# Two tokens a partition and a quartered array for the first sequence, the whole array for the others, in a fused attention and MLP kernel

## The chip, the cores and the metric

The kernel runs on one core of a Trainium2 chip. The metric is the device time of one execution in microseconds (us); lower is better. Matmul operands are bf16, sums are f32.

## The reference, cut to what matters

The inputs are q, k and v of four sequences, eight heads, 768 tokens and 64 elements a head, a decay `lam` for each head, and two weight matrices. The first stage is linear attention with decay, in blocks of tokens; the second is an MLP over the 3072 tokens with a piecewise quadratic gate.

```python
# q, k, v: (4, 8, 768, 64); w_in: (512, 2048); w_out: (2048, 512)
for b in range(nb):                         # blocks of a sequence
    intra = einsum('bhic,bhjc->bhij', qb, kb) * Dmask          # lam ** (i - j), causal
    intra = einsum('bhij,bhjd->bhid', intra, vb)
    inter = einsum('bhid,bhde->bhie', qb * lam_pow, kv_state)
    out[:, :, sl] = intra + inter
    kv_state = lam_block * kv_state + einsum('bhsd,bhse->bhde', kb * rev_pow, vb)
x = out.transpose(0, 2, 1, 3).reshape(3072, 512)
h = x @ w_in
g = where(h >= 1, h, where(h <= -1, 0, (h + 1) ** 2 / 4))
return g @ w_out
```

The kernel works with blocks of 128 tokens in place of 64, which computes the same.

## The kernel before

**Tiles.** The 3072 tokens are cut into eight stripes (`STRIPES`, line 28): stripe 0 is the first 512 tokens of sequence 0 (four blocks, C = 4), stripe 1 its last 256 (C = 2), stripes 2 to 7 are the halves of the other sequences (C = 3, 384 tokens). A unit is a stripe s and a head pair hp (two heads of 64 elements fill 128 partitions); there are four units a stripe.

**Forms.** `FORMS = "pfffwwww"` (line 27) gives each stripe its way of doing attention. In all of them decayed copies of k and q are made in bf16, k and q are transposed so that heads lie on partitions, scores are k times q for each block, they are masked, the inner products multiply them with v, a state a block is built from k and v, and the carried part multiplies q with the state before it.

- p (stripe 0): transposes by TensorE (line 344), copied out of PSUM by ScalarE (lines 352, 354); scores on half the array's rows (line 372); inner products on half its columns (line 519), carried parts on quarters of it (line 538); states by one scan on VectorE (line 468).
- f (stripes 1 to 3): transposes by TensorE too; a copy of k and v with a zero middle (`kz`, `vc`), so that inner products use the whole array and come out transposed (lines 506, 527).
- w (stripes 4 to 7): k is laid into zero-padded tiles of 128 columns a head; one DMA transposes nine tiles (`kqT<-kq`); scores, inner products and carried parts use the whole array (lines 368, 513, 532); the result has tokens on partitions (`xn`) and is turned by a second DMA (`xT<-xn`).

**The MLP.** For a stripe of T tokens, `mlp_in` (line 595) makes one of 16 column blocks of h by four matmuls of T columns; for the first three blocks of stripe 0, `mlp_in_ko` (line 609) takes one head pair at a time, so that it can begin when the first unit is done. ScalarE adds 1 and clips below at 0 (line 618), VectorE makes the gate of four blocks by three instructions (lines 575 to 577), `mlp_out` (line 627) makes 128 tokens of the output by 16 matmuls of 512 columns in four parts, ScalarE copies them out (line 635) and SP stores them. The last 128 tokens are done in two column parts (line 647).

**Loads.** q, k and v come as f32 through SP's queue, in an order of its own, one block at a time (lines 160 to 166): for k and v a partition holds one token of a block, so that each row moved is 64 f32 (256 B); for q in forms p and f a partition holds C tokens of a head side by side. Raw tiles have two buffers each for q, k and v. Weights are loaded by GpSimd's queue with a cast to bf16, w_in in four column parts (W0 to W3, line 235) and w_out in four row parts (W4 to W7, line 239).

**The order.** The program is written out by hand in `ORDER` (lines 32 to 75), a list of words; each word issues instructions to its engines, and each engine runs its own in the order of the list. So a word whose operand is late holds all that stands behind it on its engine. The words that matter here, with s the stripe and p the head pair or part:

- L load, W weight load; `@` makes a load wait for another one's landing
- k, q, v: casts with decay; the last letter is the engine (a ScalarE, d VectorE, g GpSimd)
- T, Q: transposes of k and q (in form w, T is the DMA of both); t, u: their copies out of PSUM
- S scores, s mask, R state products, r state update, O inner products and carried parts, o copy out, X the DMA that turns `xn`
- K, P: first projection (P0a is stripe 0, block 10); h its ScalarE pass; A the gate of four blocks
- Y (stripe, 128 tokens, part): second projection, y copy out, U store, Z the last one
- D: warming matmuls without use; B masks; G, J zeros; E, b, z: copies that forms p and f need

## Time and profile before

| | us |
|---|---|
| runs of the kernel: lowest, median, highest | 220.54, 220.56, 220.89 |
| span of the profiled execution | 219.9 |
| TensorE busy | 209.4 |
| VectorE busy | 148.9 |
| ScalarE busy | 125.4 |
| GpSimd busy | 60.9 |

The profile is of one execution; times in it count from the start of its span. PE is TensorE, DVE VectorE, ACT ScalarE, POOL GpSimd, and SPq the queue from which SP issues DMAs. A line of a group names line, engine, operation, output and inputs, shape and count, then busy time and mean duration in ns, then the idle time of the engine ahead of it with what ended it. A line of the time line gives start, duration and the instructions merged. A line of a window gives its bounds, its length, each engine's busy time and count, the granted clock of TensorE (1.00 is full), the mean share of 16 DMA engines (over 1 when packets overlap) and GB/s.

### The profile page before, as it was taken

The numbers are of one execution on the slowest core, as the hardware profiler recorded it, in microseconds if no ns is written. First come the engines' busy times: TensorE is split into PE (matmuls) and PEld (weight loads), VectorE is DVE, ScalarE is ACT, GpSimd is POOL, SyncE is SP. The second block draws the span as 40 slices with busy tenths as digits, with TensorE's granted clock in tenths as the row PEclk, the third lists the DMA queues.
The fourth block names the chain that finished last, engine by engine and source line by source line (L and its number), as shares of the span: only waits on it lengthen the run. The fifth ranks groups of instructions, "written<-read, shape, count | busy, mean of one in ns | idle before, by whom it ended". The sixth has DMA issues, their size and how long they took to land.

```text
span 219.9 us, 4417 instructions
## 1 busy us (share of the span) xinstructions
PE 209.4 (95%) x1667; PEld 121.0 (55%) x1667; DVE 148.9 (68%) x239; ACT 125.4 (57%) x268; POOL 60.9 (28%) x122
## 2 busy tenths in 40 slices
PE   7488999999998999999999999999999999999994
PEld 2246445446765566555655666456655565555443
DVE  1387177971998789998499489936898649346700
ACT  3675689327983576874832686326655383256320
POOL 4376036007499810430311045003600000000000
PEclk9999999999999999999999999999999999999999
DMA  4999999999999993849999999899944222310103
GB/s 123 238 233 203 206 215 191 176 221 219 232 276 231 214 192 74 206 84 255 165 202 163 167 256 151 164 243 224 210 96 97 54 66 57 145 74 23 50 22 121
DMA packets 100629, 35.95 MB, mean 163 GB/s; under 512 B 89216, under 2 KB 97664, under 8 KB 100608
## 3 DMA queue, kind: packets, MB, share of 16 engines
q1 hardware_dynamic: 96384, 31.47, 69.0%
q0 software_dynamic: 4224, 4.19, 12.2%
q8 instruction: 13, 0.21, 0.4%
q14 instruction: 8, 0.07, 0.1%
HBM read 27.27 MB, written 6.29 MB: 153 GB/s over the span
## 4 chain that ended last, share of the span: by engine, by line
PE 85%; SPq 5%; DMA 5%; ACT 2%; issue 1%; POOL 1%; DVE 0%; DVEq 0%; ACTq 0%
PE ph L595 36%; PE py L627 34%; SPq L164 3%; DMA v_nat<-in_v_dram 3%; PE ps L368 2%; DMA xT<-xn 2%; PE pk L449 2%; PE py L647 2%; PE po L506 2%; PE pt L344 1%; PE ps L372 1%; PE ph L609 1%; PE po L513 1%; PE po L532 1%; SPq L166 1%; SPq L160 1%
## 5 line engine op out<-in xcount | busy, mean ns | idle before, releaser
L618 ACT ACTIVATE tt<-ph,one 128x384 bf16<-128x384 f32 (+2 forms) x128 | 70.5, 584 | 41.1 <-PE ph L595 29.5
L595 PE MATMUL ph<-xT,w_in_sb 128*128 128x384 bf16 (+2 forms) x500 | 93.1, 325 | 0.5 <-DMA xT<-xn 0.5
L627 PE MATMUL py<-w_out_sb,gT 128*128 128x512 bf16 x368 | 87.7, 379 | 0.0
L595 PEld LDWEIGHTS <-w_in_sb 128*128 128x128 bf16 x500 | 46.5, 98 | 30.5 <-issue 0.2
L627 PEld LDWEIGHTS <-gT 128*128 128x128 bf16 x368 | 34.5, 98 | 35.0 <-DVE sz L477 0.8
L389 DVE TENSOR_TENSOR sc<-ps,mask 128x768 bf16<-128x768 f32 (+1 forms) x28 | 25.6, 914 | 11.9 <-PE ps L368 11.6
L576 DVE TENSOR_TENSOR tt<-tt,mm 128x1536 bf16<-128x1536 bf16 (+2 forms) x32 | 32.6, 1019 | 1.1
L577 DVE TENSOR_TENSOR gT<-tt,mm 128x1536 bf16<-128x1536 bf16 (+2 forms) x32 | 32.0, 998 | 1.2
L575 DVE TENSOR_SCALAR mm<-tt 128x1536 bf16<-128x1536 bf16 (+2 forms) x32 | 19.7, 616 | 18.5 <-ACT tt L618 17.7
L315 POOL TENSOR_SCALAR kq<-k_nat,dec 128x192 bf16<-128x192 f32 (+2 forms) x36 | 19.6, 556 | 24.9 <-DMA k_nat<-in_k_dram 24.8
L635 ACT COPY osb<-py 128x512 f32<-128x512 f32 x23 | 13.5, 585 | 20.4 <-PE py L627 16.0
L320 POOL TENSOR_TENSOR kq<-q_nat,dec 128x384 bf16<-128x384 f32 (+1 forms) x15 | 13.2, 891 | 28.5 <-DMA q_nat<-in_q_dram 15.2
L477 DVE SCALAR_TENSOR_TENSOR sz<-sz,lam_blk,pk 128x128 bf16<-128x128 bf16 x48 | 16.4, 347 | 3.5 <-PE pk L449 2.2
L297 POOL CAST vc<-v_nat 128x384 bf16<-128x384 f32 (+1 forms) x15 | 9.3, 629 | 31.6 <-DMA v_nat<-in_v_dram 15.6
L344 PE MATMUL pt<-ident,kq 128*128 128x128 bf16 x96 | 9.4, 220 | 3.2 <-ACT kq L311 2.4
L548 ACT CAST xn<-po 128x384 bf16<-128x384 f32 x16 | 7.7, 478 | 5.3 <-PE po L532 5.2
L550 ACT CAST xT<-po 128x384 bf16<-128x384 f32 (+2 forms) x16 | 7.5, 483 | 5.5 <-PE po L527 3.6
L475 DVE CAST sz<-pk 128x128 bf16<-128x128 f32 x12 | 3.4, 285 | 10.0 <-PE pk L449 10.0
L344 PEld LDWEIGHTS <-kq 128*128 128x128 bf16 x96 | 6.5, 98 | 6.6 <-ACT kq L311 2.9
L295 ACT CAST vc<-v_nat 128x512 bf16<-128x512 f32 (+2 forms) x9 | 4.9, 549 | 8.9 <-DMA v_nat<-in_v_dram 8.9
L352 ACT COPY kqT<-pt 128x384 bf16<-128x384 bf16 (+2 forms) x16 | 7.7, 482 | 2.6 <-PE pt L344 2.6
L583 PE MATMUL pw<-ident 128*128 128x512 bf16 x23 | 7.5, 450 | 1.4 <-POOL ident masks.py:199 1.4
(79 smaller groups left out, 163.0 us busy)
## 6 DMA issues: line engine op xcount, KB each, us to landing
out_dram<-osb SPq DMA_DIRECT2D x23, 256.0 KB, 3.0
q_nat<-in_q_dram SPq DMA_DIRECT2D x18, 256.0 KB, 4.5
k_nat<-in_k_dram SPq DMA_DIRECT2D x24, 128.0 KB, 4.7
v_nat<-in_v_dram SPq DMA_DIRECT2D x24, 128.0 KB, 4.4
k_nat<-in_k_dram SPq DMA_DIRECT2D x12, 256.0 KB, 4.9
v_nat<-in_v_dram SPq DMA_DIRECT2D x12, 256.0 KB, 5.1
w_in_sb<-in_moe_w_in_dram POOLq DMA_DIRECT2D x4, 512.0 KB, 9.3
w_out_sb<-in_moe_w_out_dram POOLq DMA_DIRECT2D x4, 512.0 KB, 9.1
```

The costliest lines, as they stand in the source:

```text
L315: nc.gpsimd.tensor_scalar(dst[:, hi, :, :], src[:, hi, :, :], dec[:, row, 2 * hp + hi:2 * hp + hi + 1], 0.0, AX.mult, AX.add)
L320: (nc.gpsimd if eng == "g" else nc.vector).tensor_tensor(dst, src, decay(row, 2 * hp, C, inner), op=AX.mult)
L344: nc.tensor.transpose(out=d["pt"][:, i, c, :], in_=d["kq"][:, i * C + c, :], identity=ident)
L389: nc.vector.tensor_tensor(out=d["sc"][:, :, 0:C, :], in0=d["ps"][:, :, 0:T].rearrange("p h (c i) -> p h c i", c=C), in1=_ins(mask[:, 2 * h ...
L477: nc.vector.scalar_tensor_tensor(out=d["ss"][:, c, :], in0=prev, scalar=lam_blk[:, hp:hp + 1], in1=kv, op0=AX.mult, op1=AX.add)
L575: nc.vector.tensor_scalar(mm, tt, 0.5, 1.0, AX.mult, AX.min)
L576: nc.vector.tensor_tensor(tt, tt, mm, op=AX.subtract)
L577: nc.vector.tensor_tensor(g[:, 4 * a:4 * a + 4, 0:T], tt, mm, op=AX.mult)
L595: nc.tensor.matmul(ph[:, 0:T], lhsT=w_in_sb[:, ko, ni * 128:(ni + 1) * 128], rhs=x_tiles[s][:, ko, 0:T], start=(ko == 0), stop=(ko == KO - 1))
L618: nc.scalar.activation(out=t_tiles[s, ni // 4][:, ni % 4, 0:T], in_=p_tiles[s, ni][:, 0:T], func=AF.Relu, bias=one[:, 0:1])
L627: nc.tensor.matmul(y_tiles[s, m], lhsT=g_tiles[s][:, ko, m * 128:(m + 1) * 128], rhs=w_out_sb[:, ko, :], start=(ko == 0), stop=(ko == FO - 1))
L635: nc.scalar.copy(out=osb, in_=y_tiles[s, m])
```

## The change

The forms become `"nnwwwwww"`, the list is new throughout, and much of the helper code is rewritten.

- **Form n** for stripes 0 and 1, the first sequence. A block of 256 tokens holds two tokens a partition, so that a row of k or v is 128 f32 (512 B). Scores, state products, inner products and carried parts are matmuls of 64 rows by 64 columns, in an order in which four neighbours lie in the four quarters of the array (`quarters`). k is not decayed; v is, while it is cast. k and q are transposed by TensorE as before. A state is made block by block in place of a scan. The inner products (word I) and the carried parts (O) are separate words; between them a memset of one element on VectorE or GpSimd (word f) waits for the last two inner matmuls, and O waits for the memset.
- **Form w** for stripes 2 to 7: two DMA transposes a unit. The masks of the two heads are two VectorE instructions in place of one.
- **Loads** carry their queue: two of k go through ScalarE's and two of v through GpSimd's at the very start, with `lam` on ScalarE's; the others go through SP's. Each load is one block. w_in is cut at column blocks 0, 3, 7, 11 and 16.
- **PSUM**: attention has four banks of one kind in place of two and one double bank; words name the pool. Copies out of PSUM name their engine.

In the new list TensorE's words begin as follows up to Y0:

```
D13m T00a D5m T01a Q00a Q01a D3m R00aa S00mm S01mm T02a Q02a R01aa T03a I00mm Q03a I01mm O00 R02aa
T10a O01 S02mm T11a Q10a R03aa S03mm Q11a I02mm R10a D1m I03am O02 S10aa R11a O03 K00 K01 K03 K02
P04 I10aa S11aa P03 O10 P08 P05 P06 P0a P0c P0f P07 P0b P09 P0d Y010 P0e R12a I11aa R13a Y000 Y011
Y001 O11 Y030 Y031 Y012 T12a Q12a T13a Q13a Y002 Y032 S12aa S13aa Y003 Y013 I12aa I13aa Y033 O13 O12
Y020 R20a Y021 S20aa R21a Y022 Y023 I20a O20 S21aa
```

VectorE's, GpSimd's and SP's:

```
DVE   q01d v00d q02d r00 s000 s001 s010 s011 f00d r01 v03d f01d q10d r02 o011d s020 s021 s030 s031 r03
      r10 f03d o020d Z4d Z3d o030d s100 r11 Z1d s101 B0d f10d s110 s111 A00 v13d q12d A01 A02 r12 A03
POOL  L001v0 L001v1 q00g v01g q03g v02g W0@L031v0 W1@L031v0 W2@L031v0 W3@L031v0 q11g v10g f02g v11g B3g
      Z2g Z0g k12g k13g W4@L122v0 W5@W3 v12g q13g k21g k22g W6@W4 W7@W4 f11g q20g q21g q22g q23g v20g
SP    L001k0 L001q0 L011k0 L011q0 L021k0 L021k1 L021q0 L011v0 L011v1 L031k0 L031k1 L031q0 L021v0 L021v1
      L031v0 L031v1 L102k0 L102q0 L102v0 L122k0@W1 L122q0 L122v0 L204k0 L204k1 L204k2 L204q0 L204q1
      L204q2 L204v0 L204v1 L204v2 T20 T21 U00 U01 T22 U03 T23 U02 X20 L304k0 L304k1 L304k2 X21
```

A load word has the stripe, the first head pair, the count of head pairs, the tensor and the block (L204k1: stripe 2, pairs 0 to 3, k, block 1). Z sets the zeros of a padded tile, F is the last output.

The core of the diff:

```diff
-FORMS = "pfffwwww"
+FORMS = "nnwwwwww"
...
-        src = src.rearrange("h (c p) d -> c p h d", p=128)
-        return [nc.sync.dma_start(out=t[:, :, c, :], in_=src[c]) for c in range(C)]
+        if FORMS[s] == "w":
+            t = t.rearrange("p (c h d) -> p c h d", h=H, c=C)
+            return [issue(out=t[:, i, h, :], in_=src.rearrange("h (c p) d -> c p h d", p=128)[i])]
...
+        t = t.rearrange("p (b h e) -> p b h e", h=H, b=C // 2)
+        return [issue(out=t[:, i, h, :],
+                      in_=src.rearrange("h (b p c) d -> b p h (c d)", p=128, c=2)[i])]
...
+W_IN = (0, 3, 7, 11, 16)
...
+    def quarters(C):
+        return [(b, c, h, h ^ x) for b in range(C // 2) for c in range(2) for x in range(2)
+                for h in range(2)]
...
+    def att_s(u, pools):
...
+        if fm == "n":
+            for b, c, h, a in quarters(C):
+                j, o = ((b * 2 + c) * 2 + a) * HD, (c * (C // 2) + b) * BLK
+                nc.tensor.matmul(ps[h][half(a), o:o + BLK], lhsT=kT[half(h), j:j + HD],
+                                 rhs=qT[half(h), (2 * b + a) * BLK:(2 * b + a + 1) * BLK],
+                                 start=True, stop=True)
+            return
...
+            nc.vector.scalar_tensor_tensor(
+                out=d["sc"][:, h, :].rearrange("p (c e) -> p c e", c=2),
+                in0=d["ps"][h].rearrange("p (c e) -> p c e", c=2),
+                scalar=dec[:, ME, 2 * hp + h:2 * hp + h + 1],
+                in1=causal_n[:, :, 0:C // 2, :].rearrange("p c b i -> p c (b i)"),
+                op0=AX.mult, op1=AX.mult)
...
-            nc.vector.tensor_tensor_scan(
-                d["ss"].rearrange("p e c -> p (e c)"), lam_z[:, hp, :],
-                d["pk"].rearrange("p e c -> p (e c)"), 0.0, op0=AX.mult, op1=AX.add)
-            return
...
+    def att_i(u, pools):
...
+            for b, c, h, a in quarters(C):
+                o = (c * (C // 2) + b) * BLK
+                d["inner"].append(nc.tensor.matmul(
+                    po[a][half(h), b * BLK:(b + 1) * BLK], lhsT=d["vs"][half(a), b, h, c, :],
+                    rhs=d["sc"][half(a), h, o:o + BLK], start=(h, a) not in seen,
+                    stop=(first and b == a == 0 and c == 1), skip_group_check=True))
...
+    def att_fence(u, eng):
+        d["fence"] = (nc.gpsimd if eng == "g" else nc.vector).memset(fence, 0.0)
+        for m in d["inner"][-2:]:
+            after(d["fence"], m)
```

More of the change, by code (lines that the diff above doesn't have):

```diff
@@ L285, in att_cast @@
-    def att_cast(u, which, eng):
+        if i < len(W_IN) - 1:
+            a, b = W_IN[i] * 128, W_IN[i + 1] * 128
+            return [nc.gpsimd.dma_start(out=w_in_sb[:, :, a:b], in_=w_in_v[:, :, a:b])]
+        i -= len(W_IN) - 1
+        a, b = W_OUT[i], W_OUT[i + 1]
+        return [nc.gpsimd.dma_start(out=w_out_sb[:, a:b, :], in_=w_out_v[:, a:b, :])]
+    kq_all = [const.tile([128, 9, 128], BF16, name=f"kq{i}") for i in range(NKQ)]
+    x_tiles, st = {}, {}
+    taken = [0]
+    fence = const.tile([1, 1], F32, name="fence")
@@ L461, in att_state, with before @@
+        d["pk"] = pk = psum(pools, "pk")[:, 0:3 * 2 * D].rearrange("p (c e) -> p c e", c=3)
+        for c in range(n):
+            for h in range(2):
+                nc.tensor.matmul(pk[:, c, half(h)], lhsT=d["kq"][:, 2 * c + h, :],
+                                 rhs=d["vc"][:, c, h, :], start=True, stop=True)
+    def before(u):
+        s, hp = u
+        if shape(s)[2]:
+            return None
+        return st[s - 1, hp]["ss"][:, after_all(s - 1) - 1, :]
     def att_state(u):
```

813 lines of the change are left out of this document (392 added, 421 removed).

## The prediction, made before the result was known

> **What bounds the kernel now.** I read the page's parts 1 and 2 first, then TensorE's waits, then the order of its work in time.
>
> ```profile
> span 219.9 us, 4417 instructions
> ...
> PE 209.4 (95%) x1667; PEld 121.0 (55%) x1667; DVE 148.9 (68%) x239; ACT 125.4 (57%) x268; POOL 60.9 (28%) x122
> ...
> PE   7488999999998999999999999999999999999994
> ```
> ```profile
> PE pk L449 <- POOL vc L297: 0.8, 2, 0.6
> PE ph L595 <- DMA xT<-xn: 0.5, 1, 0.5
> ```
>
> The page gives TensorE 95% of the span, and the slices show where the rest is: in the first four (22 us) and the last. The second fence is the whole list of TensorE's waits after 20.4 us: 1.3 us in all. So the kernel is a start of some 20 us, paced by loads and VectorE, and behind it a queue of matmuls without holes. A change can gain by a shorter queue or an earlier start, and loses whatever holes it makes. The execution profiled has 219.9 us of span; the three runs lie at 220.54 to 220.89 with a median of 220.56, so I add 0.66 to spans.
>
> Two points in time carry the argument: the first MLP matmul, and the first matmul of the second projection (Y010).
>
> ```profile
> 20.51 0.82 PE L609 MATMUL ph<-xT,w_in_sb 128*128 128x512 bf16 x3
> ```
> ```profile
> 37.97 1.24 PE L627 MATMUL py<-w_out_sb,gT 128*128 128x512 bf16 x5
> ```
>
> **What TensorE saves.** Stripes 2 and 3 (eight units, a unit being a stripe and a head pair) go from form f to form w. Both forms stand side by side in the time line (start, duration, instruction). A group's cost is the distance from its start to the next group's start.
>
> ```profile
> 74.06 0.50 PE L344 MATMUL pt<-ident,kq 128*128 128x128 bf16 x6
> 74.39 0.28 PE L449 MATMUL pk<-vc,kz 128*128 128x64 bf16 x4
> ...
> 75.37 0.81 PE L595 MATMUL ph<-xT,w_in_sb 128*128 128x384 bf16 x4
> 76.12 0.34 PE L372 MATMUL ps<-kqT 64*128 64x128 bf16 x6
> 76.39 0.82 PE L595 MATMUL ph<-xT,w_in_sb 128*128 128x384 bf16 x4
> ...
> 82.23 0.50 PE L506 MATMUL po<-sc,vc 128*128 128x128 bf16 x6
> 82.57 0.33 PE L527 MATMUL po<-kqT,sz 128*128 128x128 bf16 x3
> ```
> ```profile
> 101.71 0.50 PE L368 MATMUL ps<-kqT 128*128 128x128 bf16 x6
> 102.05 0.81 PE L595 MATMUL ph<-xT,w_in_sb 128*128 128x384 bf16 x4
> ...
> 104.21 0.34 PE L513 MATMUL po<-vc,sc 128*128 128x64 bf16 x6
> 104.38 0.28 PE L532 MATMUL po<-sz,kqT 128*128 128x128 bf16 x2
> ```
>
> Form f: transposes 0.33 (74.06 to 74.39), scores 0.27 and about 0.10 of turning to the half array before them (four L595 matmuls from 75.37 end their feeding near 76.02), inner products 0.34. Form w: no transposes, scores 0.34, inner products 0.17. States and carried parts are alike in both. So 0.33 + 0.37 + 0.34 - 0.34 - 0.17 = 0.53 us a unit, and eight units give **-4.2 us**.
>
> Stripes 0 and 1 (form n) quarter the array.
>
> ```profile
> 17.24 0.41 PE L519 MATMUL po<-sc,vc 128*64 128x128 bf16 x8
> 17.58 0.40 PE L538 MATMUL po<-kqT,ss 64*64 64x128 bf16 x6
> ```
>
> Eight half-array matmuls of 128 columns take 0.34 us, the turn to quarters included; at 0.056 apiece one after the other they would take 0.45, so pairs do run together. No row shows four quarters at once. A group of eight quarters costs 0.22 if four run together (2 x 0.056 + 0.10 for the turn) and 0.34 if two do; I take 0.28, and a second 0.10 to turn back.
> [...]
>
> **The start.** Both kernels must fill stripe 0's attention before K00, the first MLP matmul. Loads first (window, busy times, clock, DMA share, GB/s):
>
> ```profile
> 2.00:4.00 2.00, 2.00 (x7) 0.63 (x5) 0.32 (x4) 0.09 (x1) 1.23 (x3) 1.00 0.53 97
> 4.00:6.00 2.00, 2.00 (x10) 0.81 (x8) 0.60 (x4) 1.19 (x5) 0.00 (x0) 1.00 1.06 328
> 8.00:10.00 2.00, 0.81 (x12) 0.64 (x13) 0.00 (x0) 1.09 (x2) 1.20 (x3) 1.00 1.32 219
> 22.00:24.00 2.00, 2.00 (x12) 0.93 (x11) 0.00 (x0) 0.93 (x2) 0.00 (x0) 1.00 1.23 203
> ```
>
> From 4 to 6 us q moves in long rows (four tokens, 1 KB) at 328 GB/s; from 8 to 10 us k and v in rows of 256 B at 219; from 22 to 24 us weights alone at 203. Two tokens a partition make rows of 512 B, which lie between 219 and 328; I take 275. Stripe 0 then needs 1.05 MB at 328 and 2.1 MB at 275, 10.8 us from about 3 us on (97 GB/s in the first window): the last v lands at 13.8 (12.6 to 15.8 by the ends).
> [...]
>
> But loads then no longer set the start; VectorE does.
>
> ```profile
> L383 DVE SCALAR_TENSOR_TENSOR sc<-ps,dec,causal 128x512 bf16<-128x512 f32 x8 | 5.6, 740 | 0.2
> L320 DVE TENSOR_TENSOR kq<-q_nat,dec 128x512 bf16<-128x512 f32 x4 | 2.6, 685 | 0.4 <-DMA q_nat<-in_q_dram 0.4
> ```
> ```profile
> L477 DVE SCALAR_TENSOR_TENSOR sz<-sz,lam_blk,pk 128x128 bf16<-128x128 bf16 x48 | 16.4, 347 | 3.5 <-PE pk L449 2.2
> L428 DVE COPY bd<-ss 64x64 bf16<-64x64 bf16 x4 | 0.7, 184 | 0.0
> ```
>
> In the new list VectorE has, ahead of O03, the last attention group before K00: eight masks (5.6 us), two q and two v multiplications (2.7), four state rounds of four 128x64 steps, each between 184 and 347 ns (I take 0.25, so 4.0; 2.9 to 5.6 by the ends), and about 1.1 of small things (q10, one evacuation, r10, fences): 13.4 us. It starts near 6.3 us, as the q of its first multiplication is issued fourth, and waits about 1.3 us for TensorE at first. O03 comes at 21.0 and **K00 at 21.4** (20.3 to 23.0). That is later than 20.51, but half of stripe 1's transposes, scores and states and all of O03 are then done. ScalarE's two early loads and lam's cover nothing late: its first logarithm waits for lam anyway. The fences hold O alone; TensorE has other groups in between, and what they cost without that cover lies in VectorE's 1.1.
>
> **The wait that the list makes.** From K00 to Y010 the list has twelve K matmuls and twelve P blocks of four.
>
> ```profile
> 24.92 6.98 PE ph L595 x32
> 38.13 8.63 PE py L627 x40
> ```
>
> By the chain a matmul of 512 columns takes 0.218 in P and 0.216 in Y: 2.6 + 12 x 0.87 + 0.9 for I10, S11 and O10 = 14.0. TensorE is ready for Y010 at 35.4. Y010 needs W4, the first quarter of w_out.
>
> ```profile
> 13.24 2.45 POOL L235 DMA_DIRECT2D w_in_sb<-in_moe_w_in_dram  x3
> ...
> 29.69 1.49 POOL L239 DMA_DIRECT2D w_out_sb<-in_moe_w_out_dram  x2 [9.35 <-DMA k_nat<-in_k_dram]
> ```
> ```profile
> DMA to landing us min/median/max: 8.0/9.1/10.7
> ```
> ```profile
> v_nat<-in_v_dram SPq DMA_DIRECT2D x2, 128.0 KB, 8.8
> ```
>
> These are GpSimd's weight issues, the time from issue to landing of the four pieces of w_out, and that of v loads issued between 20 and 22 us, while w_in was moving. Before, W0 is issued at 13.24 and W4 at 29.69, having waited 9.35 us for k of stripe 1. After, W0 waits for v of the last head pair (about 13.4), so w_in runs at the same time as before: 2.1 MB at 203 GB/s from about 15.7, with other loads between, is in at 27. W4 waits for L122v0, which stands behind W1 (landed near 21.8) and two loads on SP. It lands when w_in lets it, at 29.5 (31.6 by the 8.8 of the last row). So W4 is issued at 29.5 and lands 8.0 to 10.7 later, 37.5 to 42.3; I take 8.7, as three loads of stripe 2 (2.4 MB on SP) now run beside it: **38.2**. TensorE stands 2.8 us. Queued behind Y010 are P0e, the rest of stripe 1 and all of Y0; on GpSimd W6 and W7 wait for W4 too, and behind them stand f11g, stripe 2's q and v, and so SP's T20 and the loads behind it.
>
> **The sum**, from Y010 to the end, against before's own: Y010 0.2 later; stripes 2 and 3 -4.2; what is left of stripe 1, +2.0 (after: eight transposes 0.45, S12 with S13 and I12 with I13 0.66 each, R12, I11 and R13 0.55, O11 0.33, O13 with O12 0.5, so 3.1; before: S13 0.3, two O of six matmuls 0.67, two R 0.1, so 1.1); P0e comes after Y010, +0.9; W6, issued only at W4's landing, +0.2; of the 1.3 us of old waits I let 0.5 go, since stripe 2 is loaded earlier. That is -1.4: **219.2 us**. Hidden under TensorE: ScalarE loses sixteen transpose evacuations, VectorE masks each head by itself (half the width twice), GpSimd loses the kz copies; all have idle time. If TensorE's cover went, VectorE's 68% would be the next bound, far off.
>
> **Rivals.** (1) *w_out in time.* If L122v0 lands by 27 and W4 in 8.0, Y010 starts at 35.4 and W6 costs nothing: 219.2 - 3.0 = 216.2. [...] Against: 8.0 is the least of four.
> (2) *DMA becomes the bound in stripes 2 and 3 (slower).*
>
> ```profile
> 38.10:60.00 21.90, 21.74 (x173) 12.86 (x171) 15.61 (x27) 12.47 (x31) 6.72 (x12) 1.00 1.03 212
> 60.00:80.00 20.00, 19.35 (x193) 12.05 (x190) 16.65 (x31) 11.56 (x27) 16.62 (x34) 1.00 1.04 232
> 80.00:100.00 20.00, 20.00 (x163) 12.35 (x163) 19.33 (x29) 14.37 (x30) 4.33 (x6) 1.00 0.64 137
> ```
> ```profile
> kqT<-kq SPq DMA_TRANSPOSE x16, 3.6
> ```
>
> Against the 1.23 to 1.32 of the loaded windows above, 38 to 80 us holds about 8 us of room. The change puts there eight kqT (0.29 MB each) and eight xT transposes (0.10), 14.4 us at 219 GB/s, and q of stripes 2 and 3 in shorter rows, 2 us; k and v of stripe 1 give back 1. So 15.4 us against 8: up to 7.4 us late, at S20 to S33, which wait for kqT (3.6 us each when the queues are quiet). From 80 us on there is room again (0.64). It decides from 1.4 us on; at half its price 222.9.
> [...]
>
> **How the numbers follow.** Forecast 0.42 (217.8 to 220.4, of it 0.37 faster and 0.05 same); rival 1 0.17; rival 2 0.30 (220.8 to 226); rival 3 0.11 (0.02 faster, 0.04 same, 0.05 slower). Within 0.2% of 220.56 (0.44 us) a measurement tells nothing from no change. Faster 0.37 + 0.17 + 0.02 = 0.56; same 0.09; slower 0.35. The range 214.8 to 224.0 leaves out rival 1 with a faster VectorE and the upper half of rival 2.
>
> **What would show it.** K00 near 21.4 with VectorE without holes before it; a hole of 2 to 3 us ahead of the first L-line of the second projection, ended by w_out's DMA; no PE transposes after stripe 1; units of stripes 2 and 3 with scores at 0.34 and inner products at 0.17; no hole over 1 us at S20 to S33. Wrong would be the forecast by a K00 after 24 us, by W4 landing beyond 40, or by kqT waits in stripes 2 and 3.

## The result: 8 us slower, and the profile after

| | before | after |
|---|---|---|
| runs: lowest, median, highest (us) | 220.05, 220.55, 220.89 | 227.31, 228.54, 230.16 |
| ratio of after to before, 95% interval | | 1.0363 (1.0316 to 1.0411) |
| span of the profiled execution (us) | 219.9 | 226.6 |
| Y010, first matmul of the second projection | 37.97 | 39.39 |
| from Y010 to the end of the last matmul | 179.02 | 182.76 |
| from there to the end of the span | 2.95 | 4.47 |

Some executions are slower than the others of the same kernel (six of the kernel before, 224.20 to 227.71 us beside 219.97 to 222.65); the medians in the tables are of all runs, the ratios of the runs without those.

The forecast was 219.2 us, with a range up to 224.0. The last three rows say where the 6.7 us between the spans lie: 1.4 ahead of Y010, 3.7 behind it, 1.5 at the end. The page of after, its span, TensorE's slices and granted clock:

```profile
span 226.6 us, 4628 instructions
...
PE   7976999999998999969999999999999999999992
...
PEclk9998599999999999996999999999999999999998
```

There are new gaps in the thirteenth and eighteenth slice (near 68 and 100 us), and the clock falls twice ahead of the end. The windows of after, cut at the clock's own steps (busy times of PE, PEld, DVE, ACT and POOL, then granted clock, DMA share, GB/s):

```profile
13.82:17.23 3.41, 2.45 (x68) 1.69 (x68) 2.41 (x9) 2.64 (x8) 3.41 (x6) 1.00 0.94 194
17.23:20.64 3.41, 1.68 (x37) 0.99 (x38) 3.00 (x9) 1.12 (x4) 1.88 (x3) 1.00 1.26 194
20.64:24.05 3.41, 3.25 (x61) 2.36 (x61) 3.30 (x15) 1.01 (x4) 1.84 (x8) 0.50 1.24 206
24.05:27.47 3.42, 3.42 (x9) 1.22 (x8) 1.76 (x8) 0.92 (x3) 0.00 (x0) 0.50 1.16 199
...
99.15:102.56 3.41, 1.36 (x16) 0.72 (x15) 0.36 (x1) 1.89 (x4) 1.53 (x3) 1.00 1.01 175
102.56:105.97 3.41, 3.41 (x21) 1.84 (x20) 2.54 (x8) 0.83 (x2) 0.00 (x0) 0.50 1.10 236
```

The windows in which TensorE was busy for 1.68 and 1.36 of 3.41 us were followed by half clock, for 6.83 and 3.41 us; the one with 2.45 us was not. In the profile of before the clock stays full from 4.1 us to 219.2, behind the last matmul at 217.0.

TensorE's time line of after at Y010, and two units of stripe 2:

```profile
36.80 2.75 PE L607 MATMUL ph<-xT,w_in_sb 128*128 128x512 bf16 x12
39.39 1.03 PE L635 MATMUL py<-w_out_sb,gT 128*128 128x512 bf16 x4
...
58.01 0.34 PE L530 MATMUL po<-vc,sc 128*128 128x64 bf16 x6
58.19 0.28 PE L559 MATMUL po<-ss,kqT 128*128 128x128 bf16 x2
58.30 0.50 PE L435 MATMUL ps<-kqT 128*128 128x128 bf16 x6
58.63 0.34 PE L482 MATMUL pk<-vc,kq 128*128 128x64 bf16 x6
```

Y010 follows without a wait. Scores cost 0.33 us (58.30 to 58.63) and inner products 0.18 (58.01 to 58.19), as the prediction had them. TensorE's two longest waits of after, what ScalarE stood for ahead of the second, and SP's issues from 84 us on:

```profile
PE ps L435 <- DMA kqT<-kq: 2.5, 2, 2.0
...
PE py L635 <- ACT tt L627: 1.3, 1, 1.3
```
```profile
67.65 0.80 ACT L334 ACTIVATE kq<-k_raw,dec 128x192 bf16<-128x192 f32 x2 [1.79 <-DMA k_raw<-in_k_dram]
```
```profile
84.22 1.20 SPq L182 DMA_DIRECT2D k_raw<-in_k_dram  x2
85.47 2.37 SPq L182 DMA_DIRECT2D q_raw<-in_q_dram  x2
87.94 4.37 SPq L578 DMA_TRANSPOSE xT<-xn  x3
92.36 0.57 SPq L182 DMA_DIRECT2D q_raw<-in_q_dram  x1
92.98 2.65 SPq L182 DMA_DIRECT2D v_raw<-in_v_dram  x3
95.73 2.67 SPq L578 DMA_TRANSPOSE xT<-xn  x1
98.50 5.62 SPq L398 DMA_TRANSPOSE kqT<-kq  x4
```

The second figure is the stretch that a line's issues fill, with any waits between them. Here there are none over 0.1 us, and behind each line the next begins at once: SP issues without a pause for 20 us. A transpose keeps it for 1.2 to 1.8 us, once for 2.67, a load for 0.6 to 1.2. The kqT that S40 waits for at 99.8 us is issued at 98.50 behind all these. The k that ScalarE stood for ahead of 67.65 us, with its relus behind it in order, was issued on SP behind X20 too.

Behind Y010 TensorE's waits sum to 4.7 us against 1.3 before, and 3.4 us at half clock cost 1.7 us. Of the 3.7 us that leaves some 1.4 us of saved work on the other side.

The end of both, after first (TensorE's last matmuls; SP's last stores, where the line at 196.07 is mostly waiting):

```profile
218.49 3.66 PE L651 MATMUL py<-w_out_sb,gT 128*128 128x384 bf16 x32
```
```profile
221.80 1.04 SPq L657 DMA_DIRECT2D out_dram<-osb  x2
222.89 0.92 SPq L644 DMA_DIRECT2D out_dram<-osb  x2
```
```profile
213.33 3.66 PE L647 MATMUL py<-w_out_sb,gT 128*128 128x384 bf16 x32
```
```profile
196.07 18.44 SPq L639 DMA_DIRECT2D out_dram<-osb  x5
216.63 1.10 SPq L656 DMA_DIRECT2D out_dram<-osb  x2
```

In before the whole rows of the last stripe are stored ahead of the last two small stores; in after they stand behind them, because the list ends `F72 U70 y71a U71`.

### The profile page after: what moved, and what is told of

Same layout as the page of the kernel before. It is cut to its first block, busy times and chain, and to the rows that moved or that the text cites. A ratio compares the mean times of both kernels' runs of the same rounds, so it can differ in the third digit from the quotient of the medians.

```text
span 226.6 us, 4628 instructions
## 1 busy us (share of the span) xinstructions
PE 212.1 (94%) x1762; PEld 120.5 (53%) x1762; DVE 153.0 (67%) x273; ACT 117.4 (52%) x242; POOL 78.8 (35%) x119
## 4 chain that ended last, share of the span: by engine, by line
PE 53%; DMA 27%; DVE 5%; SPq 5%; issue 3%; POOL 2%; ACT 2%; ACTq 0%; POOLq 0%; DVEq 0%
PE py L635 23%; PE ph L607 22%; DMA w_out_sb<-in_moe_w_out_dram 6%; DMA q_raw<-in_q_dram 6%; DMA v_raw<-in_v_dram 5%; DMA k_raw<-in_k_dram 4%; DMA w_in_sb<-in_moe_w_in_dram 3%; DMA kqT<-kq 3%; PE ps L435 3%; DVE tt L594 2%; SPq L182 2%; DVE gT L595 2%; PE py L651 2%; SPq L398 1%; ACT tt L627 1%
## 5 line engine op out<-in xcount | busy, mean ns | idle before, releaser
L336 POOL TENSOR_SCALAR kq<-k_raw,dec 128x192 bf16<-128x192 f32 x34 | 19.2, 583 | 63.9 <-DMA k_raw<-in_k_dram 49.7
L452 DVE TENSOR_TENSOR sc<-ps,mask 128x384 bf16<-128x384 f32 x48 | 24.5, 550 | 20.0 <-PE ps L435 19.8
L284 POOL TENSOR_TENSOR kq<-q_raw,dec 128x384 bf16<-128x384 f32 x24 | 29.7, 1264 | 10.3 <-DMA q_raw<-in_q_dram 9.2
L593 DVE TENSOR_SCALAR mm<-tt 128x1536 bf16<-128x1536 bf16 (+2 forms) x32 | 20.5, 642 | 18.6 <-ACT tt L627 17.2
L279 ACT COPY osb<-py 128x512 f32<-128x512 f32 (+1 forms) x24 | 13.6, 580 | 37.5 <-PE py L635 34.6
L506 DVE SCALAR_TENSOR_TENSOR ss<-ss,lam_blk,pk 128x128 bf16<-128x128 bf16 (+1 forms) x64 | 20.9, 329 | 5.9 <-PE pk L482 4.2
L435 PE MATMUL ps<-kqT 128*128 128x128 bf16 x144 | 11.8, 219 | 2.5 <-DMA kqT<-kq 2.5
L435 PEld LDWEIGHTS <-kqT 128*128 128x128 bf16 x144 | 9.5, 98 | 5.2 <-DMA kqT<-kq 3.1
L281 POOL CAST vc<-v_raw 128x384 bf16<-128x384 f32 x14 | 9.5, 710 | 3.7 <-DMA v_raw<-in_v_dram 2.8
L530 PEld LDWEIGHTS <-sc 128*128 128x128 bf16 x144 | 7.4, 100 | 2.9 <-DVE ss L506 0.2
L445 DVE SCALAR_TENSOR_TENSOR sc<-ps,dec,causal_n 128x256 bf16<-128x256 f32 (+1 forms) x15 | 8.2, 594 | 0.9 <-PE ps L429 0.9
```

Source lines behind the costliest of these rows:

```text
L279: nc.scalar.copy(out=o, in_=i)
L284: (nc.gpsimd if eng == "g" else nc.vector).tensor_tensor(o, i, f, op=AX.mult)
L336: (nc.gpsimd if eng == "g" else nc.vector).tensor_scalar(o, i[:, :, h, :], f, 0.0, AX.mult, AX.add)
L435: nc.tensor.matmul(ps[h][:, c * BLK:(c + 1) * BLK], lhsT=d["kqT"][:, 2 * c + h, :], rhs=qT[:, c * BLK:(c + 1) * BLK], start=True, stop=True)
L452: nc.vector.tensor_tensor(out=d["sc"][:, h, :].rearrange("p (c i) -> p c i", c=C), in0=d["ps"][h].rearrange("p (c i) -> p c i", c=C), in1= ...
L506: nc.vector.scalar_tensor_tensor(out=d["ss"][:, c, :], in0=prev, scalar=lam_blk[:, hp:hp + 1], in1=kv, op0=AX.mult, op1=AX.add)
```

## The experiments

**Theory** after these readings: three separate causes, namely SP's queue in stripes 2 and 3 (3.7 us), the late w_out (1.4), the order of the last stores (1.5). **Rivals**: the DMA engines are the bound there (as the prediction had it); or the half clock is what costs. All kernels, each timed beside the kernel before on the same chip; the last four columns are from the profiled executions (of two kernels only the times are used). "Half" is the time at half clock between 28 us and the last matmul:

| kernel | median us | ratio to before (95%) | Y010 | Y010 to last matmul | behind it | half |
|---|---|---|---|---|---|---|
| before | 220.55 | | 37.97 | 179.0 | 3.0 | 0 |
| changed | 228.54 | 1.036 (1.032 to 1.041) | 39.39 | 182.8 | 4.5 | 3.4 |
| c1_changed | 229.06 | 1.036 (1.032 to 1.041) | 38.92 | 184.9 | 4.5 | 3.4 |
| e1_loads_first | 230.06 | 1.039 (1.032 to 1.045) | 39.49 | 184.7 | 4.5 | 0 |
| e2_keep_clock | 230.37 | 1.042 (1.034 to 1.051) | 41.42 | 185.1 | 4.5 | 3.4 |
| e3_no_act_queue | 229.25 | 1.035 (1.028 to 1.041) | 40.29 | 183.3 | 4.5 | 6.8 |
| e4_warm_wait | 230.03 | 1.039 (1.032 to 1.046) | 40.39 | 184.5 | 4.5 | 0 |
| e5_loads_on_act | 232.75 | 1.055 (1.050 to 1.060) | 38.60 | 187.6 | 4.5 | 6.8 |
| e6_plain_copies | 224.65 | 1.019 (1.014 to 1.024) | 39.23 | 178.7 | 4.5 | 0 |
| e8_early_y | 231.70 | 1.049 (1.039 to 1.059) | 40.65 | 186.0 | 4.5 | 3.4 |
| e9_both | 238.12 | 1.079 (1.072 to 1.086) | 39.65 | 193.5 | 4.4 | 10.2 |
| e10_stores_first | 228.38 | 1.033 (1.028 to 1.038) | 39.13 | 184.4 | 3.0 | 3.4 |
| e11_w_alone | 250.02 | 1.132 (1.126 to 1.137) | 37.41 | 207.8 | 2.9 | 20.5 |
| e12_w4_first | 230.43 | 1.043 (1.039 to 1.047) | 38.46 | 187.2 | 2.9 | 6.8 |
| e13_w_third | 234.01 | 1.058 (1.053 to 1.062) | | | | |
| e14_split_copies | 237.82 | 1.077 (1.072 to 1.083) | 38.68 | 193.0 | 4.5 | 6.8 |
| e15_k30_later | 227.80 | 1.031 (1.028 to 1.035) | 39.20 | 183.8 | 3.0 | 3.4 |
| e16_s40_later | 229.16 | 1.037 (1.033 to 1.041) | 39.14 | 184.5 | 2.9 | 3.4 |
| e17_loads_on_pool | 251.99 | 1.129 (1.123 to 1.136) | | | | |
| e18_pool_and_order | 250.67 | 1.139 (1.130 to 1.149) | 39.74 | 202.9 | 3.0 | 20.5 |

**Order of the loads.**

```diff
-L304k0:s ... L304v2:s            spread behind X20
+L304k0:s ... L304v2:s X20        all ahead of it; L404q2, L404v0 to v2 ahead of X30
```

> The changed kernel with only the place of some loads in the list altered: all loads of stripe 3 stand ahead of X20, and q (third piece) and v of stripe 4 ahead of X30, so that on SP's queue no load stands behind a transpose that waits for ScalarE's xn. Theory A (one queue in order): the holes of 0.66 us at 77 us and of 2.21 us at 99 us, where the scores wait for kqT, go, and with the second the stretch at half clock at 102 to 106 us, worth 1.7 us; also part of the 1.47 us at 67 us. 3 to 5 us less than the changed kernel: 223.5 to 225.5. Rival B (DMA is the bound in stripes 2 and 3, as the prediction's rival had it): the loads land no earlier or push X and kqT back, the holes only move: 227.5 to 229.

Theory A failed: no gain, and a span of 228.7 us within rival B's range. X20 is issued 11 us later (71.03 against 59.53), T30 at 76.77 against 74.62, and SP issues without a pause all the same. Whatever stands first, SP's list is as long. The half clock behind S40 did not come, and Y010 to the last matmul is not shorter than in the control (184.7 and 184.9 us): the clock alone does not set the time.

**The half clock.**

```diff
-        for j in range(C):
+        for j in list(range(C)) * (4 if i == 1 and u in ((1, 0), (1, 1)) else 1):
```

> The changed kernel with the eight q transposes of the first two head pairs of stripe 1 issued four times over (repeated work, the same result): 24 more matmuls of 128 columns, 1.3 us of TensorE, at 18.0 and 19.8 us, where it waited for VectorE. Theory A (the clock gate counts TensorE's idle time): the stretch from 17.2 to 20.6 us, half idle before, is now over 80% busy, and the 6.8 us at half clock from 20.64 on do not come. K00 about 0.5 us earlier, and the twelve K matmuls at 0.22 instead of 0.43 us. TensorE is then ready for Y010 near 36.5 us and waits for w_out's first piece, which lands at 39.2 whatever the clock is: little at the end, 0 to 0.5 us less, 227.8 to 228.5, with a new hole of 2 to 3 us ahead of Y010. Rival B (the early loss adds up to the end): 2.5 to 3.4 us less, 225 to 226. Rival C (the half clock comes from something else): clock and time stay, 228.5 to 229.5.

None of the theories was tried as meant. The edit added twelve matmuls and not 24, since these units have two q transposes each, and half clock came all the same, in another place. The windows of that kernel:

```profile
12.17:15.59 3.42, 2.34 (x63) 1.63 (x63) 3.35 (x9) 2.66 (x5) 2.78 (x4) 1.00 1.20 294
15.59:19.00 3.41, 1.87 (x46) 1.36 (x42) 2.12 (x8) 1.80 (x6) 3.41 (x6) 0.50 0.89 141
```

The grid of 3.41 us stands elsewhere in this execution (15.59 where the changed kernel has 20.64), and another stretch, 2.34 us busy and ahead of the added matmuls (18.96 us on), was the one that half clock followed. So windows that were 40% (1.36 us) and 69% (2.34 us) busy both had half clock behind them.

```diff
-Y213 y20a S40aa
+Y213 y20a D9m S40aa
```

> The changed kernel with nine warming matmuls of 512 columns (1.9 us, results unused) ahead of S40, in the hole of 2.21 us at 99.4 us, where S40 waits for kqT. Theory A (half clock after a half idle stretch): the hole stays in size but is busy, the stretch at half clock from 102.6 to 106.0 us does not come: 1.5 to 1.8 us less, 226.6 to 227.0. Rival B (the half clock has nothing to do with the hole, or the loss there is made good later): the same time within 0.4 us.

The stretch at half clock behind S40 did not come, so the first half of theory A holds. The time did not follow: Y010 to the last matmul is 184.5 us, as in the control's 184.9, and a pause of 1.3 us ahead of a gate stands at 124 us, where the control has 0.4. Rival B.

**ScalarE's queue.**

```diff
-L001k1:a L011k1:a | L001v0:g L001v1:g | D13m L001k0:s L001q0:s L011k0:s L011q0:s
+| L001v0:g L001v1:g | D13m L001k0:s L001q0:s L011q0:s L001k1:s L011k0:s L011k1:s
...
-    nc.scalar.dma_start(out=lam_b, in_=lam.partition_broadcast(128))
+    nc.sync.dma_start(out=lam_b, in_=lam.partition_broadcast(128))
```

> The changed kernel with the two k loads and the load of lam that it issues on ScalarE's queue issued on SP instead (lam first, then k, q, q, k, k, k of the first two head pairs). Theory A: the time outside the span, 1.7 us in the changed kernel and 0.65 before, comes from a third queue in use, and falls to about 0.7: the time is 227.3 to 227.8 if the span stays at 226.6. Rival B: the time outside the span has nothing to do with that queue and stays at 1.7. Apart from that the start may shift by up to 0.5 us either way, since three issues of 0.4 to 0.5 us each are added to SP.

Rival B: 1.7 us stay outside the span, and beside it the kernel before has 1.7 too (220.89 us with a span of 219.2, 220.68 with 219.0). This kernel also answers what the half clock at the start costs, as it had none there. TensorE at Y010:

```profile
34.70 2.32 PE L607 MATMUL ph<-xT,w_in_sb 128*128 128x512 bf16 x10
40.29 1.31 PE L635 MATMUL py<-w_out_sb,gT 128*128 128x512 bf16 x4 [3.27 <-DMA w_out_sb<-in_moe_w_out_dram]
```

TensorE was ready at 37 us and stood 3.27 us for W4: the prediction's wait, which in the changed kernel lies hidden behind 6.8 us at half clock. So the half clock at the start takes the place of a wait that would have come anyway.

**Loads off SP, to ScalarE; transposes out; an earlier Y010; both.**

```diff
-L304k0:s ... L404v2:s
+L304k0:a ... L404v2:a            q2, v0 to v2 of stripe 4 also some 6 us earlier
```

> The changed kernel with the eighteen loads of stripes 3 and 4 issued on ScalarE's queue instead of SP's (q's third piece and v of stripe 4 some 6 us earlier in the list). In the changed kernel SP issues without a pause from 84.2 to 104.2 us: a transpose keeps it for 1.2 to 1.5 us, a load for 0.45 to 1.2. Theory A (SP's issuing is the bound from 60 to 104 us): SP is freed of about 9 us there, T30 is issued about 2 us earlier and T40 about 5 us earlier, the holes of 0.66 us at 77 and 2.21 us at 99 us go, and the 1.47 us at 67 us shrinks, as k30 no longer waits for a load issued behind X20: a span of 222 to 224. Rival B (the DMA engines are the bound; SP's issues are long because the queue is full): the holes stay within 1 us in sum, 226 to 228. Rival C (ScalarE becomes late by its eighteen issues of 0.45 us): holes ahead of P and Y that end with ScalarE's relu, 227 to 229.

Rival C, and beyond its 227 to 229: a span of 230.7 us. ScalarE's queue in that kernel:

```profile
89.03 2.31 ACTq L182 DMA_DIRECT2D v_raw<-in_v_dram  x2
```

Issues of loads keep ScalarE for 1.2 us each here and up to 1.9 elsewhere, relus and xn copies stand behind them, and SP stands for xn: the four X of stripe 2 take it 15.4 us, of which their issues are 4.8. The load's issue has moved to an engine with less room.

```diff
+        if u[0] in (2, 3):
+            nc.sync.dma_start(out=turned(u)[:, 0:3 * C, :], in_=kq_of(u)[:, 0:3 * C, :])
+            return
...
+        if s in (2, 3):
+            nc.sync.dma_start(out=x_tiles[s][:, hp, :], in_=st[u]["xn"])
+            return
```

> The changed kernel with the sixteen DMA transposes of stripes 2 and 3 (eight kqT, eight xT) replaced by plain DMA copies of the same bytes between the same tiles: what it leaves out is the transposing itself, so stripes 2 and 3 come out with other values. A plain copy should keep SP for about 0.5 us instead of 1.2 to 1.5 and move rows of 768 and 2304 B. Theory A (these transposes, by SP's time or by that of the DMA engines, make the holes from 60 to 104 us): all holes there that end with kqT go, 3 to 4.5 us of span: 222 to 223.5, and SP no longer issues without a pause. Rival B (the loads and ScalarE's order make the holes): no more than 1 us gained.

Theory A. Y010 to the last matmul falls to 178.7 us, 4.1 less than in the changed kernel's profile and 6.2 less than in the control's; no half clock there, no wait for kqT. Two of SP's issues of copies, in that kernel:

```profile
55.61 0.47 SPq L398 DMA_DIRECT2D kqT<-kq  x1
...
72.69 2.63 SPq L398 DMA_DIRECT2D kqT<-kq  x3
```

The three copies of the second line keep SP for 0.5 us each; the rest of the 2.63 us is waiting for casts. So the sixteen transposes cost what was lost behind Y010. Whether by SP's time (mostly 0.5 us for each instead of 1.2 to 1.4) or by the engines', this kernel can't tell.

```diff
+TIMES = {"Q03": 2, "R02": 3, "T10": 3, "T11": 4, "Q10": 4, "Q11": 4}   # words issued so often
...
-W4@L122v0
+W4@W3
```

> The changed kernel with two things for the start: transposes and one state group repeated in TensorE's pauses between 13 and 21 us (repeated work, the same result), against the half clock; and W4 made to wait for W3 instead of the v load of stripe 1, which it waited for until 31.7 us, so that it is issued when W3 lands near 29.5 us. Theory A (Y010 is set by the later of TensorE, 36.6 us at full clock, and W4): W4 lands at 37 to 37.5 us and Y010 starts there, 2 us earlier; if nothing behind it is bound otherwise, the span falls by 2 us to 224.5. Rival B (from 60 us on the queue of loads and transposes sets the pace): Y010 is earlier by 2 us but the holes from 67 to 104 us grow by 1.5 to 2 us: 226 to 227.

Neither. No half clock up to 40 us, TensorE ready at 38.0, but W4 was issued only at 33.3 and landed at 40.5: on GpSimd it stands behind the casts k12g and k13g, which wait for a load (30.8) and took 2.4 us. Here the casts held it, not L122v0.

> The two kernels before this one in a single one: repeated transposes at the start, W4 behind W3, and the loads of stripes 3 and 4 on ScalarE's queue. Theory A (Y010 at 37.3 us and SP freed): 220 to 221.5 of span, level with the kernel before. Rival B (the DMA engines are the bound): 225 to 227. Rival C (ScalarE late by its issues): 226 to 228.

Worse than the sum of its parts: the pauses behind Y010 end with w_out's third piece, ScalarE's relus, the scores' banks and the gates.

**The last stores, and W4 ahead of the casts.**

```diff
-y70a F72 U70 y71a U71
+y70a U70 y71a U71 F72
```

> The changed kernel with the last words of its list in the order that the kernel before has: U70 and U71 (the stores of the first two token blocks of the last stripe) ahead of F72 (matmuls, copies and stores of the third). In the changed kernel U70 and U71, whose data are ready 4 us earlier, are issued at 222.9 us, behind F72's two stores, and from TensorE's last matmul to the end of the span go 4.7 us, against 3.1 before. Theory A (the stores stand behind F72 on SP's queue): 3.1 to 3.3 us after the last matmul, 1.4 to 1.6 us less: a span of 224 to 227 beside 225.5 to 228.4 of the changed kernel. Rival B (the last two stores take as long wherever the others stand): no change behind the last matmul.

Theory A for the tail: 3.0 us behind the last matmul instead of 4.5. SP's end in that kernel:

```profile
219.78 2.02 SPq L644 DMA_DIRECT2D out_dram<-osb  x2
223.14 1.04 SPq L657 DMA_DIRECT2D out_dram<-osb  x2
```

The median hardly shows it, since Y010 to the last matmul varies by 2 us between executions (182.8 and 184.9 for the same kernel).

```diff
-k12g k13g o100a ... W4@L122v0 h05
+W4@W3 k12g k13g o100a ... h05
```

> The kernel with the stores in the old order, and besides W4 (w_out's first piece) ahead of the two k casts of stripe 1 on GpSimd's queue and made to wait for W3 instead of stripe 1's v load. Theory A (W4 is late because it stands behind casts that wait for loads): it is issued at 29.5 us instead of 32, lands near 37, and Y010 starts when TensorE is ready: 37.5 where the clock stays full, 39 where it is half for 6.8 us. 0 to 2 us less than the kernel with the stores alone. Rival B (what is gained at Y010 is lost where the scores of stripes 3 and 4 wait for kqT): the same span within 0.5 us, with larger holes from 67 to 104 us.

W4 is issued at 30.05 and lands at 37.80, Y010 is 0.7 us earlier than with the stores alone, and the gain is lost at once: TensorE then stands 3.2 us for a relu at 39.5 us.

**Form w alone, on the list of before.**

```diff
-FORMS = "pfffwwww"
+FORMS = "pfwwwwww"               T, X, zeros placed as the casts and copies allow
```

> The kernel before with one part of the change alone: stripes 2 and 3 in form w (DMA transposes, whole array), on the list of before, with the PE transposes and kz copies left out, T where the later of the two casts is done, X behind each evacuation, and zeros written into five kq tiles earlier. Theory A (the prediction's sum: TensorE saves 0.53 us a unit, and the DMA transposes are hidden): 4 us less than before, 216.5. Rival B (the prediction's rival 2: DMA transposes among the loads make holes at S20 to S33 and at the first projection): holes of 4 to 10 us in sum between 50 and 105 us that end with kqT or xT; 220 to 227. Part of these can come from the list, which gives T of stripe 2 only some 4 us before its scores.

> The kernel before with stripe 3 alone in form w, edited in the same way. Theory A (all hidden): 2 us less, 218.5. Rival B: holes of 2 to 5 us between 70 and 105 us; 219.5 to 223. If half of the DMA transposes costs clearly less than half of what both stripes cost, the load of the DMA engines decides; if it costs half, each transpose has its price.

Rival B, and far beyond its numbers: 29 us and 13 us slower. TensorE's waits with both stripes:

```profile
PE ps L368 <- DMA kqT<-kq: 17.1, 4, 7.4
PE ph L595 <- DMA xT<-xn: 5.9, 8, 1.4
```

On a list that was not arranged for them the transposes cost several times what TensorE saves. One stripe costs somewhat under half of two. Part of it is the list's, as the expectation says; the sum is no measure of the transposes alone.

**The control, and the cause inside.**

> The changed kernel once more, unaltered, beside the next three on the same chip. Its span was 225.5 to 228.4 us in four executions, and holes and half clock from 60 to 106 us differ between executions of kernels that do the same there. Theory: the same spread again, 225.5 to 228.5, and 1.7 us outside the span for it and for the kernel before alike.

As expected; spans of 227.0 to 228.2 us.

```diff
+            for j in range(0, 3 * C, C):
+                nc.sync.dma_start(out=turned(u)[:, j:j + C, :], in_=kq_of(u)[:, j:j + C, :])
...
+            for j in range(0, 384, 128):
+                nc.sync.dma_start(out=x_tiles[s][:, hp, j:j + 128], in_=st[u]["xn"][:, j:j + 128])
```

> As the kernel with plain copies in place of the sixteen DMA transposes of stripes 2 and 3 (it leaves out the transposing, so stripes 2 and 3 have other values), but each copy in three pieces of the same bytes in all, so that SP issues about 1.4 us for each, as for a transpose (1.2 to 1.5), while the DMA engines move plain rows. Theory A (the time that the DMA engines take for transposes makes the holes; queue q1 took 167 us of the engines in the changed kernel and 155 us with plain copies): as with plain copies, a span of 222 to 223.5. Rival B (SP's time for issuing makes them): the holes come back, 225.5 to 227.5.

Rival B, the one that speaks for SP, and slower than its 225.5 to 227.5. The same bytes in plain rows, and 13 us slower than in whole copies. Queue q1's share of the engines, in the changed kernel, with plain copies and with split ones:

```profile
q1 hardware_dynamic: 105680, 34.09, 73.7%
```
```profile
q1 hardware_dynamic: 95184, 34.09, 69.6%
```
```profile
q1 hardware_dynamic: 99792, 34.09, 65.8%
```

Of 226.6, 222.4 and 236.2 us that is 167, 155 and 155 us of engine time. The engines do no more with split copies than with whole ones, and they have room. One of the 10 us windows, DMA share second to last:

```profile
80.00:90.00 10.00, 8.85 (x94) 6.01 (x93) 7.21 (x15) 5.47 (x11) 0.00 (x0) 1.00 0.61 187
```

From 50 to 100 us these shares are 0.61 to 1.03, against 0.90 to 1.25 in the changed kernel. It is SP that does more:

```profile
78.37 5.70 SPq L399 DMA_DIRECT2D kqT<-kq  x9
...
92.28 6.25 SPq L584 DMA_DIRECT2D xT<-xn  x9
```

A unit's three pieces keep SP for 1.9 to 2.1 us here. Summed over the sixteen units, SP is kept for 32.8 us by the split copies, 29.7 by the transposes of the changed kernel and 12.6 by the whole copies, and 32 more issues bring a gap of 0.05 to 0.1 us each. Of the 55 us from 50 to 105, all of SP's issues take 40.9 in the kernel before, 50.8 in the changed one, 40.4 with whole copies and 49.8 with split ones. Y010 to the last matmul is 8 us longer than in the control, 1.7 us of it by half clock. SP's time for issuing sets the pace from 50 to 105 us.

```diff
-s231 k30a k31g ... k33g h1e
+s231 k31g ... k33g h1e k30a
```

> The kernel with the stores in the old order, and k30 (ScalarE's cast of stripe 3's first k, which waits for a load) moved in ScalarE's order from ahead of six relus to behind them. Theory A (Y100's hole of 1.5 to 2.7 us at 67 us is ScalarE standing at k30): the hole goes, with a stretch at half clock where there was one; 3 us less than the changed kernel with the 1.4 us of the stores: 223 to 225 of span. Rival B (what is gained there is lost at the scores of stripe 3 and 4, which wait for kqT): 225 to 227.

The hole at 67 us goes, but 2.0 us come at 77, where P20 waits for xT:

```profile
77.21 0.32 PE L607 MATMUL ph<-xT,w_in_sb 128*128 128x384 bf16 x1 [2.02 <-DMA xT<-xn]
```

The best version that leaves no transposing out, 227.80 us against the control's 229.06 on the same chip: about what the stores give. Rival B.

```diff
-Y213 y20a S40aa U20 R40a y21a Y223 s400 s401 U21 R41a P30
+Y213 y20a U20 y21a Y223 P30 S40aa R40a s400 s401 U21 R41a
```

> The same kernel as the one before it, and S40 moved behind Y223 and P30, which gives TensorE 1.5 us of work while S40's kqT is under way. Theory A: the hole of 1.1 to 2.2 us at 99 to 105 us shrinks to under 0.7 us, and no stretch at half clock follows it: 1.5 to 3 us less again, 221 to 223 of span. Rival B (the transposes and loads set the pace, and the wait moves to the next scores): less than 0.7 us gained.

Rival B: S40's wait falls to 0.6 us and TensorE stands 2.2 us at 115 us, for a relu. The holes at 67 and 99 us are places where one common lateness shows.

```diff
-L304k0:s ... L404v2:s
+L304k0:g ... L304v2:g            behind v23g
+L404k0:g ... L404v2:g            behind v33g
```

> The changed kernel with the eighteen loads of stripes 3 and 4 issued on GpSimd's queue, where it idles: stripe 3's behind the last v cast of stripe 2 (near 55 us; GpSimd stands from there to 67.7 us in the changed kernel), stripe 4's behind the last v cast of stripe 3 (near 77 us; it stands to 89.5). Theory A (SP's issuing is what makes stripes 2 and 3 late; the split copies, with the engines' bytes unchanged and SP's time raised, cost 14 us): SP loses 18 issues of 0.45 to 1.2 us between 60 and 96 us, T30 is issued 2 to 3 us earlier and T40 5 us or more, the holes at 67, 78 and 100 us go, 4 to 5 us less than the changed kernel: a span of 222 to 224. Rival B (a third of the same work on another queue brings nothing, since the DMA engines are shared): 226 to 228.5, with SP's transposes taking longer to land than 3.4 us. [...]

> The same loads on GpSimd's queue, in the kernel with the stores in the old order and k30 later. Theory A: 1.4 us less than the kernel before it by the stores, and none of the holes at 67 us: 220.5 to 222.5, still 1 to 3 us above the kernel before, since Y010 stays at 39 us and the holes at W6 and at VectorE's gates stay. Rival B: 224.5 to 226.5, as without the loads moved.

Both failed by more than any theory gave. In the second kernel GpSimd issues nine loads in 8 us, and SP's transposes beside them take long to land:

```profile
PE ps L435 <- DMA kqT<-kq: 15.9, 4, 8.8
```
```profile
66.61 18.03 SPq L578 DMA_TRANSPOSE xT<-xn  x4
84.75 16.93 SPq L398 DMA_TRANSPOSE kqT<-kq  x3
```

The kqT issued at 55.70, 59.16 and 84.75 us land 10.7, 16.6 and 14.0 us later, where those of the changed kernel take 3.2 to 5.5 in stripes 2 and 3 once the first is through. From 61.4 to 64.8 us the DMA share is 1.20 at 150 GB/s, against 0.94 at 192 from 61.6 to 65.0 us in the changed kernel. That one queue in order protects the transposes, because SP's issuing spaces the loads out, is the author's estimate from these numbers; no run varied the spacing alone.

**Settled**: the transposes of stripes 2 and 3 cost what was lost behind Y010 (plain copies), SP's issuing is how the changed kernel pays for them (split copies), and the order of the stores costs 1.5 us. **Open**: whether any arrangement gets under both limits. No run takes time off SP with the transposes left in and nothing else made late, so that gain is not shown. No version beat the kernel before.

## Why the prediction was wrong, point by point

- **Bound now.** The reading held, the base didn't: "I add 0.66 to spans" took the profiled execution for one like those timed. Later runs of both kernels have 1.7 us outside the span, and spans of before lie at 218.3 to 220.9 us, most near 219; the profiled 219.9 was an execution about 1 us longer than these. This is 1.1 us of the error.
- **What TensorE saves.** Right: 0.33 and 0.18 us for scores and inner products, no PE transposes behind stripe 1. With the transposes out, Y010 to the last matmul is 0.3 us shorter than before, though its waits behind Y010 sum to 2.2 us against 1.3: about 1.2 us less work, where -4.2 + 2.0 + 0.9 gave 1.3.
- **Quarters** (rival 3, the array not quartered, at 0.11). All four run together:

```profile
29.20 0.31 PE L522 MATMUL po<-sc,vs 64*64 64x128 bf16 x8
29.33 0.28 PE L429 MATMUL ps<-kqT 64*64 64x128 bf16 x8
29.55 0.82 PE L607 MATMUL ph<-xT,w_in_sb 128*128 128x512 bf16 x3
```

  Eight inner products in 0.13 us, where one after the other, at 0.056, they would take 0.45; scores with the turn back in 0.22: less than the 0.28 taken. No run shows the loss that rival 3 reckoned with; the group with the turn costs 0.09 more than the one without.
- **The start.** The loads held: the last v of stripe 0 lands at 14.49 us for 13.8, and the windows from 4 to 13.8 us have 294 to 329 GB/s, above the 275 taken. VectorE's work was right (12.9 us busy from 8.2 to 23.4 us, for 13.4), its start wasn't:

```profile
8.23 0.69 DVE L284 TENSOR_TENSOR qn<-q_raw,dec 128x512 bf16<-128x512 f32 x1 [2.15 <-DMA q_raw<-in_q_dram]
```

  "It starts near 6.3 us" priced the fourth issue on SP and not the five loads that two other queues put beside it; with three of them on SP's queue instead (**ScalarE's queue** above) the same multiplication starts at 6.97 us. Behind the start VectorE stood 0.5 and 1.2 us more for q, where no hole was forecast. K00 came at 23.89 instead of 21.4, and by the text's own mark (24) just short of wrong.
- **W4.** The mechanism held: issued at 31.95 instead of 29.5, it landed at 39.16 instead of 38.2, within its bounds. That it is so near is partly luck: it was issued 2.4 us late and took 7.2 us, less than the 8.0 of the lower bound. The hole did not show, because TensorE was late itself by K00 and by half clock. L122v0, landing at 31.67, held it in the changed kernel; without that condition GpSimd's casts did (33.3), and ahead of both it went at 30.05.
- **The sum behind Y010.** The failed step: "stripes 2 and 3 -4.2" was taken whole, with nothing for the time that their sixteen transposes keep SP; the stretch behind Y010 came out 3.7 us longer where the sum had 1.6 us less. Rival 2, at 0.30, had the wait (kqT) and nearly the place right (to S33; the longest wait was S40's), and its resource wrong: it counted the bytes of the DMA engines, whose share was lowest from 40 to 110 us, 0.93 and 0.90, in the 10 us with the hole at 68 us and in those ahead of the hole at 100 us, and never the time of SP. The result lies beyond its 226, too. SP's time could be read in the trace of before, where the later stripes' transposes mostly keep it for 1.2 to 1.5 us each. Sixteen more are some 20 us of an engine that also issues most loads and all stores (29.7 us as they came), and the kernel before left 14 us of SP's time from 50 to 105 us. A row of before, from SP's issues, and the changed kernel's windows with the holes (DMA share second to last):

```profile
84.65 2.92 SPq L336 DMA_TRANSPOSE kqT<-kq  x2
```
```profile
60.00:70.00 10.00, 8.69 (x98) 7.41 (x96) 7.76 (x17) 7.38 (x19) 2.26 (x6) 1.00 0.93 191
...
90.00:100.00 10.00, 9.78 (x53) 4.44 (x51) 5.59 (x7) 2.12 (x5) 6.01 (x9) 1.00 0.90 157
```

- **The end.** No step priced the last words of the list, though the kernel shows them: 1.5 us.
- **The clock** was quoted as 1.00 throughout and taken as given. Behind Y010 it cost 1.7 us in the profile, and less than that in the end: where it stayed full, other waits took its place.

The errors sum up: 1.2 at Y010, 5.3 behind it (a forecast of -1.6, a result of +3.7), 1.5 at the end and 1.1 of base are 9.1 us, from 219.2 to the profiled run's 228.33.

## What to carry to other kernels

Where a change moves work to DMA, price three things: the engines' bytes, the landing, and the issuing engine's time for each DMA, with everything that stands in order behind it; the rows of the issuing queue in the old trace give the last. Read the end of a hand-written list as closely as its start. When a hole's removal brings no time, look for the queue that is as long as before instead of for the next hole.

## What the runs showed of the hardware

- **The granted clock** changed on a grid of 3.41 us in each of the sixteen traces read in such windows, and the grid stood elsewhere from one to another: half clock began at 20.64 us in the changed kernel, at 18.35 in c1_changed, at 15.59 in e2_keep_clock. Behind 28 us, sixteen windows at full clock had TensorE busy for up to 1.36 us, and each was followed by half clock; of those with 1.48 us or more none was. At the start, among small matmuls, windows with 1.60 to 2.58 us were followed by half clock, and others with 1.67 (the kernel before, from 7.55 us) or more were not. So the busy time alone does not decide there; what does is open.
- **A DMA transpose against a plain copy** of the same 288 KB (medians): issue to landing 3.4 and 3.3 us, SP kept 1.3 and 0.5 us; queue q1's time on the engines, with eight kqT and eight xT of the one or the other, 167 and 155 us. The landings agree; the time of the issuing queue and that of the engines do not.
- **A queue's issue** is not of one length. In e5_loads_on_act a load on ScalarE's queue kept it for 0.4 to 0.6 us from 60.5 to 64.3 us, where the DMA share was 0.89 (60.3 to 63.7 us), for 1.2 in the mean of the two from 89.0 to 91.3 us, where it was 1.06 (87.6 to 91.0), for 1.9 from 91.4 to 93.3 us, where it was 1.32 (91.0 to 94.4), and for 0.4 at 68.5 us, where it was 1.12 (67.1 to 70.5); the share alone does not set it. A kqT transpose of the changed kernel kept SP for 1.2 us at its shortest and 4.5 at its longest; with nine loads of GpSimd's queue under way (e18_pool_and_order) three of them filled 16.9 us, any waits between them included.
